# A recurrent outer-product layer with a maxout network on one core: a new list of steps, output weights in packets of two rows, GpSimd steps tied to the list, and the last span's operands turned by transfers

## Chip, core and metric

The kernel runs on one core of a Trainium2 chip. The metric is the device time of one execution in microseconds, as the median of several runs. Engines are named as in the profile: PE (TensorE), PEld (its weight loads), DVE (VectorE), ACT (ScalarE), POOL (GpSimd), SP (SyncE, which here issues the transfers). Each takes its instructions from its own queue, in order. Matmuls write PSUM, which has 8 banks here, each of 512 float32 in 128 partitions.

## What is computed

Four batches, eight heads, 768 time steps, 48 features a head. A gated recurrence makes y; its heads side by side (384 columns) are the input of a small network:

```python
f = 1.0 / (1.0 + np.exp(-f_logit))
for t in range(S):
    state = f[:, :, t, :, None] * state + np.einsum('bhd,bhe->bhde', k[:, :, t], v[:, :, t])
    y[:, :, t] = np.einsum('bhd,bhde->bhe', q[:, :, t], state)
x = y, as 3072 rows of 384
out = np.maximum(x @ w1, x @ w2) @ w_out      # w1, w2: 384 x 1024, w_out: 1024 x 384
```

Everything is float32 in memory. The kernel uses max(a, b) = relu(a - b) + b: with wd = w1 - w2 and m2 = w2 @ w_out, out = relu(x @ wd) @ w_out + x @ m2.

## The kernel before

Time is cut into three windows of 256 steps, each in two halves of 128 steps, and a "span" s (0 to 11) is one window of one batch: window s // 4, batch s % 4. A partition holds two neighbouring time steps (the "parities"), so 64 partitions hold a half. Of each span four arrays f, k, q, v are loaded, 384 KB each, into 27 slots of one tile (line 122, packets of 384 bytes: two steps of one head).

The whole program is a list of words, `ORDER` (lines 20 to 58). The loop in lines 541 to 543 takes each word apart into a step, its numbers, the engine (a, v, p, s for ACT, DVE, POOL, SP) and the PSUM bank after the @, and calls the step's function. So the list gives each engine the order of its queue. What one engine needs of another is a semaphore wait that the framework derives from the tiles. The instructions stay in the list's order; nothing plans again at build time.

The steps of one span, in the order of the data:

- Lf, Lk, Lq, Lv: the loads (SP). E, F, G: the gate's exponential and logarithm (ACT, lines 211 to 221). e: sum of the two parities' logarithms (line 223). C: running sums by a triangular matmul (PE, line 226). X, Z: their exponentials (ACT).
- i, j: k and q of the even step times the gate. K, Q: keys and queries scaled to the start of the half, in bf16 (lines 257, 260). V: cast of v (line 264). These run on DVE or POOL, V also on ACT.
- t, u: 16 + 16 transposes of keys (t) and queries (u) on PE (line 268) into two banks. U: their copy to SBUF, tile `trs` (line 279).
- A: keys times queries within a half (line 284). m: that product times the causal mask, on DVE (line 297). D: the state that a half adds (line 378). n, N: the state after a half and its decay (lines 401, 408).
- S, z, y: PE adds what the state gives (S, line 327) and what the half itself gives (y, line 359) in two banks; z is a one-column copy by DVE in between, so that PE and DVE agree on S's end.
- Y: copy of y to SBUF. For spans 0 to 5 and 11 y is written transposed (tile `xT`). Spans 6 to 10 ("TURNED") write it untransposed into `xr`, of which there is one buffer, and M (line 425) is a transposing transfer on SP that makes `xT`.
- d0 to d3: x @ wd, 6 matmuls each (line 431). r: relu to bf16, tile `gT` (line 439). o: the output for one parity, 3 matmuls with m2 and 8 with w_out (line 449). b: copy of the result to SBUF. O: the store (line 468), for TURNED spans two transfers.

The weights have their own steps. Wa0 to Wa3: quarters of w1's columns, 384 KB each. Wb0 to Wb2: rows of w2, 512 KB each. Wo0, Wo1: halves of w_out, 768 KB each. ws: one quarter of wd, w1 - w2 (line 509), which needs all of w2. wc, wt, wx: cast, transpose and copy of w2. wo: casts of w_out. wm, wn: m2 and its copy. g: zeroes of a state buffer.

The list lets PE begin with spans 0 and 1 and the weights; then spans follow each other with the steps of neighbours interleaved.

Of the kernel before, what the change touches and what calls it, by code (L numbers as in the profile page):

```python
# [27 lines left out]
wo2p wo3a d1.1@3 r1.1v@6 Z2 wm0@0 X2 g6v Lk4s@22 r1.0a@2 i2v wm1@1 K2v Lf5s@23 j2v wm2@2 Q2v Lq4s@24  # L28
E3 wn1v@1 t2@4 u2@4 F3 U2.0v@4 Lf6s@12 V2p wn2a@2 wn0v@0 o0.1@1 U2.1v@5 e3p A2.1@2 Lq5s@13 b0.1.0a@1
D2@4 A2.0@6 G3 n2.0v C3@0 j3v o1.1@1 Z3 n2.1v Lk5s@0 i3v X3 Q3v o1.0@0 m2.1v@2 E4 K3p F4 m2.0v@6  # L30
b1.1.0a@1 S2.0@2 V3p u3@4 z2v@2 t3@4 e4p S2.1 y2 U3.2v@4 D3@6 Y2.2a@2 C4@1 n3.0v N2.1v A3.0@4 G4
n3.1v A3.1@2 m3.0v@4 E5 o0.0@6 i4p F5 m3.1v@2 Z4 d2.2@4 X4 e5v G5 j4v S3.0@2 b0.0.0a@6 d2.3@5 K4v E6
O0.2s C5@1 Lq6s@1 d2.1@7 z3v@2 r2.1a@4 Q4v Lv4s@2 S3.1 y3 Lk6s@3 F6 j5v Lf7s@4 N3.1v t4@4 X5 Y3.2v@2
i5p u4@4 Lv6s@5 Z5 d2.0@6 U4.2v@4 e6p d3.1@3 r2.0a@6 d3.0@2 g7p K5v G6 C6@1 d3.2@4 r3.0a@2 Q5v
d3.3@5 Z6 j6v X6 t5@2 u5@2 Q6v r3.1a@4 o2.1@1 U5.2v@2 V4a i6p b1.0.0a@0 O1.2s A4.1@2 K6p D4@4
m4.1v@2 A4.0@6 Lv5s@6 E7 o3.1@0 Lf8s@7 F7 Lq7s@8 n4.0v m4.0v@6 Lf9s@9 N4.0p e7p Lq9s@10 t6@2
# [12 lines left out]
r7.0a@4 N9.0v i10p Lv10s@24 d8.3@7 O6.2s X10 d8.1@5 r7.1a@2 K10v d8.2@6 d8.0@4 r8.1a@6 o7.1@1
r8.0a@4 j10v Q10p S9.0@2 t11@4 t10@6 z9v@2 u11@4 S9.1 y9 U11.0v@4 u10@6 U11.1v@5 o7.0@0 U10.2a@6  # L50
V11v V10v b7.1.0v@1 o8.1@4 Y9.2a@2 b7.0.0a@0 M9s D10@1 b8.1.0a@4 D11@0 O7.2s A11.0@2 A10.0@6 n11.0v
A11.1@4 m10.0v@6 o8.0@0 m11.1v@4 d9.0@6 N11.0v n10.0v d9.1@7 m11.0v@2 N10.0p d9.3@5 r9.0a@6 d9.2@4
b8.0.0v@0 O8.2s S10.0@0 r9.1a@4 S11.0@2 z10v@0 A10.1@6 z11v@2 S11.1 y11 m10.1v@6 S10.1 y10 Y11.0a@2
Y11.1a@3 o9.0@4 Y10.2a@0 M10s d11.2@5 b9.0.0v@4 d11.1@0 d11.3@1 o9.1@4 d10.1@3 b9.1.0v@4 r11.4a@5
# [6 lines left out]
M2_LAST = (0,)  # L61
TURNED = (6, 7, 8, 9, 10)


@with_exitstack
def kernel(
# [196 lines left out]

    def step_V(s, e):
        copy(e, pad("vb", s)[:, :, :, 0:D], by_parity(loaded[s]["v"]))


    def transposes(s, x, b):
        src = pad("kpqp"[2 * x:2 * x + 2], s)
        for j in range(NP):  # L270
            for par in range(2):
                for h in range(2):
                    rows = slice(h * HC, (h + 1) * HC)
                    ps = banks16[:, b + h, :].rearrange("p (x j a t) -> p x j a t", x=2, j=NP, a=2)
                    nc.tensor.transpose(out=ps[:, x, j, par, :],  # L275
                                        in_=src[rows, par, 2 * j:2 * j + 2, :].rearrange("p r e -> p (r e)"),
                                        identity=ident[rows, rows])
# [49 lines left out]
    def step_S(s, part, b):  # L327
        t = tr[s]
        if s in TURNED:
            ys[s] = b if part == 0 else ys[s]  # L330
            for j in range(NP):
                for r in range(2):
                    h = r if part else 1 - r
                    if has_state(s, h):
                        rows = slice(r * DP, r * DP + D)
                        add_turned(s, h, 2 * j + r, t[rows, h, 1, j].rearrange("p a t -> p (a t)"),
# [131 lines left out]
    def step_O(g, part):  # L468
# [3 lines left out]
        if g in TURNED:  # L472
            dst = out[row:row + W, :].rearrange("(h t a) m -> a t h m", h=2, a=2)
            for a in range(2):
                nc.sync.dma_start(out=dst[a], in_=obs[g][a * HC:(a + 1) * HC])
            return
        if g == n_s - 1 and part > 0:
            cols = slice((part - 1) * HD // 2, part * HD // 2)
            nc.sync.dma_start(out=dst[:, 1, cols], in_=obs[g][:, 1, cols])
            return  # L480
        pars = slice(0, 2) if part == 2 else slice(part, part + 1)
        nc.sync.dma_start(out=dst[:, pars, :], in_=obs[g][:, pars, :])


    def cast_w2(kt, e):
        copy(e, w2b[:, kt, :], w2_f[:, kt, :])
# [22 lines left out]
    def subtract(part, e):  # L509
        cols = slice(part * d_ff // 4, (part + 1) * d_ff // 4)  # L510
        engines[e].tensor_sub(wd[:, :, cols], w1_f[:, :, cols], w2_f[:, :, cols])
# [13 lines left out]
        "t": lambda s, e, b: transposes(s, 0, b), "u": lambda s, e, b: transposes(s, 1, b),  # L525
        "U": lambda s, i, e, b: step_U(s, i, e, b),
# [3 lines left out]
        "Y": lambda s, i, e, b: step_Y(s, i, e, b), "g": lambda i, e, b: step_g(i, e), "M": lambda s, e, b: step_M(s, e),  # L530
        "D": lambda s, e, b: step_D(s, b),
# [3 lines left out]
        "O": lambda s, i, e, b: step_O(s, i),  # L535
# [38 lines left out]
```

## Time and profile before

| what | us |
| --- | --- |
| median of three runs | 140.69 (140.13, 140.69, 142.11) |
| the profiled execution | 141.23 |
| its span, first to last instruction | 139.5 |
| busy PE, PEld, DVE, ACT, POOL | 119.1, 89.5, 101.7, 79.0, 45.3 |
| transfers: bytes, mean rate over the span | 29.65 MB, 213 GB/s |

The profile is of one execution. Its times count from the first instruction of the span, in microseconds; the 1.73 us between span and time lie outside. In a timeline row come start, duration, engine, line, operation, tiles and count, and in square brackets how long the engine had been idle and what ended that. In a row by form come the total busy time, the mean of one in nanoseconds, and the idle time ahead of such instructions. A row of stretches gives the stretch, its length, the busy time of the five engines, the granted clock, the share of the 16 DMA engines and GB/s. PE's busy time is modelled in part, since matmuls are pipelined: a busy PE may not be at its peak.

### The profile page before, as it was taken

The page shows a single profiled execution, that of the slowest core. Times are in us where ns is not written, and L with a number is a line of the kernel's source. Part 1 is how long each engine was busy: PE and PEld are TensorE (multiplying, and loading weights), DVE is VectorE, ACT ScalarE, POOL GpSimd, SP SyncE. Part 2 cuts the span into 40 slices and gives each one's busy share as a digit, 9 for nine tenths or more (in the row PEclk, how much of TensorE's full clock was granted, in tenths as well). Part 3 has the DMA queues.
Part 4 walks back from the last instruction along what each step waited for, and adds up shares of the span by engine and source line. Part 5 has one row for each costly group of instructions (what it writes and reads, how often), then busy time and mean ns, then how long its engine had stood idle before and what let it go on. Part 6 is the DMA issues. An engine that isn't in the chain of part 4 may idle for free. (4 is left out here: it accounts for less than half of the span.)

```text
span 139.5 us, 5551 instructions
## 1 busy us (share of the span) xinstructions
PE 119.1 (85%) x2455; PEld 89.5 (64%) x2455; DVE 101.7 (73%) x173; ACT 79.0 (57%) x120; POOL 45.3 (32%) x52
## 2 busy tenths in 40 slices
PE   0045489599999999999999699989999999999991
PEld 0024377586567687677787566776877668778671
DVE  5687798999889999989974989982642768312630
ACT  3784349665592996973983355693675814504301
POOL 5003007640538224482073096719635001000000
PEclk9999999999999999999999999999999999999999
DMA  4999999999999989999999999909899461422124
GB/s 109 271 261 296 348 332 349 369 267 251 269 265 257 271 222 273 239 248 250 247 297 222 224 274 163 288 30 96 121 260 313 130 140 34 118 56 61 57 62 164
DMA packets 59768, 29.65 MB, mean 213 GB/s; under 512 B 54368, under 2 KB 58592, under 8 KB 59744
## 3 DMA queue, kind: packets, MB, share of 16 engines
q1 hardware_dynamic: 59744, 29.30, 87.5%
q8 instruction: 19, 0.31, 1.0%
q14 instruction: 5, 0.04, 0.1%
HBM read 23.59 MB, written 4.72 MB: 203 GB/s over the span
## 5 line engine op out<-in xcount | busy, mean ns | idle before, releaser
L436 PE MATMUL banks<-xT,wd 128*128 128x256 bf16 x288 | 34.7, 273 | 2.3 <-DVE xT L114 2.0
L461 PE MATMUL banks<-wo,gT 128*128 128x384 bf16 (+1 forms) x200 | 35.3, 320 | 0.0
L436 PEld LDWEIGHTS <-wd 128*128 128x128 bf16 x288 | 27.2, 98 | 6.9 <-issue 2.3
L445 ACT ACTIVATE gT<-banks 128x1024 bf16<-128x1024 f32 (+1 forms) x20 | 19.5, 982 | 20.2 <-PE banks L436 15.7
L299 DVE TENSOR_TENSOR at_m<-banks,mask 128x1024 bf16<-128x1024 f32 x24 | 28.8, 1218 | 0.8 <-PE banks L292 0.5
L461 PEld LDWEIGHTS <-gT 128*128 128x128 bf16 x200 | 19.2, 98 | 11.8
L247 POOL TENSOR_TENSOR slots<-slots,one 128x384 f32<-128x384 f32 x8 | 8.5, 1058 | 28.1 <-DMA slots<-in_k_dram 18.3
L461 PE MATMUL banks<-m,xT 128*128 128x384 bf16 (+1 forms) x75 | 15.9, 320 | 0.0
L114 ACT COPY ob<-banks 128x384 f32<-128x384 f32 (+1 forms) x16 | 7.4, 460 | 11.9 <-PE banks L461 11.9
L114 DVE COPY trs<-banks 128x2048 bf16<-128x2048 bf16 (+1 forms) x12 | 11.9, 997 | 2.4 <-PE banks L275 2.3
L213 ACT ACTIVATE gate<-slots 128x768 f32<-128x768 f32 x12 | 10.1, 841 | 5.0 <-DMA slots<-in_f_logit_dram 5.0
L114 DVE COPY ob<-banks 128x384 f32<-128x384 f32 x9 | 5.0, 555 | 8.9 <-PE banks L461 8.9
L228 PE MATMUL banks<-e,u_inc 128*128 128x384 bf16 x12 | 4.2, 354 | 8.0 <-DVE e L224 8.0
L258 POOL TENSOR_TENSOR kp<-slots,inv 128x768 bf16<-128x768 f32 x5 | 9.6, 1913 | 3.0 <-DVE slots L247 2.9
L404 DVE TENSOR_TENSOR tmp_s<-banks,state 128x192 f32<-128x192 f32 x16 | 5.6, 352 | 6.7 <-ACT ob L114 3.9
L217 ACT ACTIVATE ell<-gate 128x768 f32<-128x768 f32 x12 | 10.1, 845 | 0.2
L292 PE MATMUL banks<-trs 48*64 48x128 bf16 x384 | 10.1, 234 | 0.0
L261 POOL TENSOR_TENSOR qp<-slots,dec 128x768 bf16<-128x768 f32 x4 | 7.3, 1817 | 8.3 <-PE banks L314 4.9
L251 DVE SCALAR_TENSOR_TENSOR slots<-gate,slots 128x384 f32<-128x384 f32 x12 | 6.6, 552 | 3.9 <-DMA slots<-in_q_dram 3.9
L114 ACT COPY trs<-banks 128x1024 bf16<-128x1024 bf16 (+1 forms) x4 | 4.8, 1227 | 7.0 <-PE banks L275 7.0
L292 PEld LDWEIGHTS <-trs 48*64 48x64 bf16 x384 | 7.5, 115 | 1.6 <-issue 1.1
L461 PEld LDWEIGHTS <-xT 128*128 128x128 bf16 x75 | 6.5, 97 | 3.2
(73 smaller groups left out, 186.3 us busy)
## 6 DMA issues: line engine op xcount, KB each, us to landing
slots<-in_f_logit_dram SPq DMA_DIRECT2D x12, 384.0 KB, 6.4
slots<-in_q_dram SPq DMA_DIRECT2D x12, 384.0 KB, 6.2
slots<-in_k_dram SPq DMA_DIRECT2D x12, 384.0 KB, 6.1
slots<-in_v_dram SPq DMA_DIRECT2D x12, 384.0 KB, 5.8
out_dram<-ob SPq DMA_DIRECT2D x6, 384.0 KB, 3.9
out_dram<-ob SPq DMA_DIRECT2D x11, 192.0 KB, 3.4
slots<-in_moe_w_dram SPq DMA_DIRECT2D x4, 384.0 KB, 8.7
slots<-in_moe_w_dram SPq DMA_DIRECT2D x3, 512.0 KB, 8.8
```

Of the source, the lines that this page charges most:

```text
L114: (nc.scalar.copy if e == "a" else engines[e].tensor_copy)(out, in_)
L213: nc.scalar.activation(flat(gate[s]), flat(loaded[s]["f"]), AF.Exp, bias=0.0, scale=-1.0)
L217: nc.scalar.activation(flat(ell[s]), flat(gate[s]), AF.Ln, bias=1.0, scale=1.0)
L247: engines[e].tensor_mul(even, even, one[s])
L251: engines[e].scalar_tensor_tensor(out=even, in0=gate[s][:, :, 1, :], scalar=1.0, in1=even, op0=ALU.add, op1=ALU.mult)
L258: engines[e].tensor_mul(pad("kp", s)[:, :, :, 0:D], by_parity(loaded[s]["k"]), both(inv[s]))
L261: engines[e].tensor_mul(pad("qp", s)[:, :, :, 0:D], by_parity(loaded[s]["q"]), both(dec[s][:, 0:HD].rearrange("p (h d) -> p h d", h=H)))
L292: nc.tensor.matmul(out=ps[h * HC:(h + 1) * HC, j % 2, par, :], lhsT=t[rows, h, 0, j, par, :], rhs=t[rows, h, 1, j].rearrange("p a t -> p ( ...
L299: nc.vector.tensor_mul(at[s][:, jj].rearrange("p r j a t -> p (r j) (a t)"), banks[:, b:b + 2, :].rearrange("p r (j x) -> p (r j) x", j=2) ...
L436: nc.tensor.matmul(out=ps[:, f], lhsT=wd[:, kt, ff * C:(ff + 1) * C], rhs=xT[g][:, kt], start=(kt == 0), stop=(kt == KT - 1))
L445: nc.scalar.activation(dst, src, AF.Relu)
L461: nc.tensor.matmul(out=ps, lhsT=lhs, rhs=rhs, start=(i == 0), stop=(i == len(terms) - 1))
```

## The change

All of `ORDER` is new, 578 words for 574. What it does:

- The loads at the start come as f0, f1, k0, Wb2, q0, q1, v0, f2, Wb0, Wb1, k1, Wa1, Wa0, v1, Wa3, Wa2, Wo1, f3, Wo0 (before: f0, f1, q0, k0, k1, v0, q1, Wa2, Wb1, v1, Wb2, Wb0, f2, Wa0, Wa3, Wa1, Wo0, Wo1). The steps behind them are rearranged; those for keys of span 0 now come ahead of its queries.
- Steps change engine. For instance DVE makes 8 of the K (7 before), 10 of the e (6), 7 of the i (4), 7 of the N (9), and 6 of the U copies (12); ACT makes 10 of the U (4), all wn and five of the V (3); POOL has 2 of the e (6), 5 of the i (8), 4 of the K (5), 9 of the N (7) and 2 of the ws (1).
- The queries of spans 0 and 1 are made by halves of the heads (q), turned by halves (uq), and copied in parts (U with numbers 3 to 5: all keys, the first or the second half of the queries).
- The output weights are loaded with two neighbouring rows in one packet of 3072 bytes (1536 before). So partition p of a pair of feature blocks holds features 2p and 2p + 1, and w1 and w2 have to be dealt in the same way: `cast_w2` and `subtract` read every second column.
- A step of the kinds in `SHARED` on POOL gets a dependency on the last listed step of these kinds on DVE.
- Span 11's keys and queries are turned by two transfers on SP (Mk, Mq, 256 KB each) in place of t11, u11 and two U11 copies; A11 and S11 read the other layout.
- O7, O8, O9 and the last part of O11 are issued by ACT.

```diff
 ORDER = """
-Lf0s@16 g0v Lf1s@17 Lq0s@18 Lk0s@19 Lk1s@20 Lv0s@21 Lq1s@22 Wa2s E0 Wb1s F0 Lv1s@23 E1 e0v C0@0 F1
-Wb2s j0v Z0 e1v X0 Q0v G0 C1@1 Wb0s i0v X1 u0@2 G1 g2v K0v Lf2s@24 i1p t0@2 U0.0v@2 U0.1a@3 Wa0s V0v
-Z1 K1v D0@2 A0.1@0 Wa3s j1v A0.0@4 Q1v Wa1s m0.1v@0 u1@6 t1@6 Wo0s n0.0v U1.0a@6 U1.1a@7 Wo1s V1v
-n0.1v D1@0 m0.0v@4 S0.0@2 A1.0@6 Lk2s@25 wc2a z0v@2 m1.0v@6 A1.1@4 S0.1 y0 Lq2s@26 wc0a ws2p n1.0v
-n1.1v m1.1v@4 S1.0@6 Y0.0a@2 wt2@0 Lf3s@16 E2 g5p z1v@6 N1.1v S1.1 y1 N0.1p Lv2s@17 g3p ws0v wt0@1
-Y1.1a@7 wx2a@0 Y0.1v@3 wc1p Lq3s@18 Y1.0v@6 d0.2@2 F2 g1p ws3v d0.0@4 Lk3s@19 wx0a@1 wt1@0 g4v e2v
-d0.3@3 ws1v C2@1 r0.1a@2 d1.2@6 Lf4s@21 wo0v wx1v@0 wo1p d0.1@5 G2 d1.3@7 r0.0v@4 d1.0@2 Lv3s@20
...
+Lf0s@16 g5p g7v g3v Lf1s@17 g2p Lk0s@18 g0p Wb2s Lq0s@19 Lq1s@20 Lv0s@21 Lf2s@22 E0 Wb0s F0 Wb1s E1
+e0v C0@0 F1 Lk1s@23 G0 X0 i0v G1 Wa1s wc2v Z0 K0v e1v Wa0s t0@0 j0v wt2@2 U0.3v@0 Lv1s@24 q0.0v C1@3
+j1v uq0.0@0 q0.1v Wa3s V0v uq0.1@0 U0.5a@0 wx2v@2 U0.4a@0 A0.1@4 Z1 Wa2s A0.0@0 m0.1v@4 X1 q1.0p E2
+Wo1s g6p q1.1v m0.0v@0 g4p uq1.1@2 uq1.0@2 U1.5a@2 wc0p D0@4 Lf3s@25 F2 n0.0v S0.0@0 Wo0s z0v@0 i1p
+n0.1v S0.1 y0 N0.1p Lq2s@26 K1v wt0@4 Y0.1a@1 wc1a U1.4v@2 ws1v t1@2 wt1@5 U1.3a@2 e2v Lk2s@16 ws0v
+C2@6 wx0a@4 A1.1@2 Y0.0v@0 Lv2s@17 V1p wx1v@5 d0.0@0 m1.1v@2 d0.1@1 Lk3s@18 ws3p A1.0@4 r0.0a@0 D1@2
+m1.0v@4 Lq3s@19 Z2 ws2p d0.3@1 G2 n1.0v X2 n1.1v S1.0@4 z1v@4 S1.1 y1 Lv3s@21 wo2v d0.2@0 Y1.0v@4
+Y1.1a@5 wo3p Lf4s@22 E3 d1.3@3 d1.1@5 F3 d1.2@2 e3v d1.0@4 Lf5s@20 wo1a wo0v C3@7 r0.1v@0 r1.0a@4
...
 M2_LAST = (0,)
+SHARED = ("e", "i", "j", "K", "Q", "q", "V", "N", "ws", "wc", "wo")
 TURNED = (6, 7, 8, 9, 10)
+BY_DMA = (11,)
...
-        engines[e].dma_start(out=wo_f[:, part, :],
-                             in_=moe_w_out.rearrange("(j p) m -> p j m", p=C)[:, part, :])
+        engines[e].dma_start(out=wo_f[:, part, :].rearrange("p (g two) m -> p g (two m)", two=2),
+                             in_=moe_w_out.rearrange("(g p two) m -> p g (two m)", p=C, two=2)[:, h * FG // 4:(h + 1) * FG // 4, :])
...
+    def step_q(s, jj, e):
+        hs = slice(4 * jj, 4 * jj + 4)
+        sums = dec[s][:, 0:HD].rearrange("p (h d) -> p h d", h=H)[:, hs]
+        engines[e].tensor_mul(pad("qp", s)[:, :, hs, 0:D], by_parity(loaded[s]["q"])[:, :, hs],
+                              sums.unsqueeze(1).to_broadcast([C, 2, 4, D]))
...
     def step_U(s, part, e, b):
         t = tr[s] = buf("trs", s, 3, [C, 2, 2, NP, 2, HC], BF16)
+        if part > 2:
+            x, js = (0, slice(0, NP)) if part == 3 else (1, slice(2 * part - 8, 2 * part - 6))
+            src = banks16[:, b:b + 2, :].rearrange("p h (x j y) -> p h x j y", x=2, j=NP)
+            copy(e, t[:, :, x, js].rearrange("p h j a t -> p h (j a t)"),
+                 src[:, :, x, js].rearrange("p h j y -> p h (j y)"))
+            return
...
+    def step_turn(s, x, e):
+        t = tr[s] = buf("trs", s, 3, [C, 2, 2, NP, 2, HC], BF16)
+        src = pad("kpqp"[2 * x:2 * x + 2], s).rearrange("p two h e -> p (two h e)")
+        engines[e].dma_start(out=whole(t)[:, x], in_=src, transpose=True)
...
     def cast_w2(kt, e):
-        copy(e, w2b[:, kt, :], w2_f[:, kt, :])
+        copy(e, w2b[:, kt, :].rearrange("p (g f m) -> p g f m", f=2, m=C),
+             w2_f[:, kt, :].rearrange("p (g m f) -> p g f m", f=2, m=C))
...
     def subtract(part, e):
         cols = slice(part * d_ff // 4, (part + 1) * d_ff // 4)
-        engines[e].tensor_sub(wd[:, :, cols], w1_f[:, :, cols], w2_f[:, :, cols])
+        w1, w2 = (t[:, :, cols].rearrange("p k (m f) -> p k f m", f=2) for t in (w1_f, w2_f))
+        engines[e].tensor_sub(wd[:, :, cols].rearrange("p k (f m) -> p k f m", f=2), w1, w2)
...
+    ahead = None
     for word in ORDER.split():
         key, of, e, b = re.fullmatch(r"([A-Za-z]+)([0-9.]+)([avps]?)@?([0-9]*)", word).groups()
         steps[key](*map(int, of.split(".")), e, int(b or 0))
+        if key in SHARED and e in ("v", "p"):
+            ins = nc.cur_bb.bb.instructions[-1]
+            if e == "v":
+                ahead = ins.name
+            elif ahead:
+                tc.add_manual_dep(ins, ahead, mybir.DependencyInfo(mybir.DependencyClass.Sync,
+                                                                   mybir.DependencyReason.DATA),
+                                  reason="as listed")
```

The queue of DVE in the new list from the first weight cast to the end of span 1 is: wc2, K0, e1, j0, U0.3, q0.0, j1, q0.1, V0, wx2, m0.1, q1.1, m0.0, n0.0, z0, n0.1, K1, U1.4, ws1, e2, ws0, Y0.0, wx1, m1.1, m1.0, n1.0, n1.1, z1. PE's, up to the point of which the prediction speaks: C0, t0, wt2, C1, uq0.0, uq0.1, A0.1, A0.0, uq1.1, uq1.0, D0, S0.0, S0.1, y0, wt0, t1, wt1, C2, A1.1, d0.0, d0.1, A1.0, D1, d0.3, S1.0, S1.1, y1, d0.2.

Later in the list, PE's queue behind span 10's y is o9.1, S11.1, y11, o9.0, d10.2; and between K11 and A11.1 it has D9, A9, o7.0, the four d8, S9, y9, o7.1, A10.1 and D11.

More of the change, by code (lines that the diff above doesn't have):

```diff
@@ L31 @@
[L31 to L36, printed above, removed]
@@ L49 @@
[L49 to L54, printed above, removed]
@@ L58 @@
+r9.0a@4 N10.0v b8.0.0a@2 S10.0@0 S11.0@4 z10v@0 A11.0@6 S10.1 y10 m11.0v@6 o9.1@2 Y10.2a@0 z11v@4
+b8.1.0a@3 M10s S11.1 y11 b9.1.0a@2 O8.2a o9.0@3 Y11.0v@4 Y11.1v@5 d10.2@0 b9.0.0a@3 d10.1@5 d10.0@4
+d11.1@2 r10.0a@4 d11.3@3 O9.2a d10.3@1 d11.0@4 r10.1v@0 d11.2@5 o10.0@6 r11.4a@5 r11.2a@4 r11.3a@2
+r11.5a@3 o10.1@5 b10.0.0v@6 o11.0@2 b10.1.0v@5 O10.2s o11.1@3 b11.0.0v@2 O11.0s o11.2@2 b11.1.1v@3
+O11.1s b11.1.2a@2 O11.2a
 """
 M2_LAST = (0,)
+SHARED = ("e", "i", "j", "K", "Q", "q", "V", "N", "ws", "wc", "wo")
@@ L335, in step_S @@
                         rows = slice(r * DP, r * DP + D)
+                        if s in BY_DMA:
+                            for a in range(2):
+                                nc.tensor.matmul(
+                                    out=banks[a * HC:(a + 1) * HC, ys[s] + h, (2 * j + r) * D:(2 * j + r + 1) * D],
+                                    lhsT=query_t(s, rows, h, j)[:, a], rhs=heads_of(state_before(s, h))[rows, j, :],
+                                    start=(s, h, a) not in begun, stop=False, skip_group_check=True)
+                                begun.add((s, h, a))
+                            begun.add((s, h))
+                            continue
                         add_turned(s, h, 2 * j + r, t[rows, h, 1, j].rearrange("p a t -> p (a t)"),
```

86 lines of the change are left out of this document (51 added, 35 removed).

## The prediction

> **What bounds the kernel now.** I read the page's busy shares and slices first, then busy time in chosen stretches, then the timeline of the first 30 us, and last the rows by form and the times to landing.
>
> ```profile
> PE 119.1 (85%) x2455; PEld 89.5 (64%) x2455; DVE 101.7 (73%) x173; ACT 79.0 (57%) x120; POOL 45.3 (32%) x52
> ...
> PE   0045489599999999999999699989999999999991
> ...
> GB/s 109 271 261 296 348 332 349 369 267 251 269 265 257 271 222 273 239 248 250 247 297 222 224 274 163 288 30 96 121 260 313 130 140 34 118 56 61 57 62 164
> ```
>
> TensorE is filled from about the ninth slice on; in the first eight it is not. In stretches (columns: length, then busy us of PE, PEld, DVE, ACT, POOL):
>
> ```profile
> 0.00:28.51 28.51, 13.63 (x370) 11.82 (x371) 23.12 (x55) 16.30 (x23) 7.89 (x19) 1.00 1.07 293
> 28.51:90.00 61.49, 59.79 (x1308) 43.57 (x1306) 55.87 (x86) 40.96 (x66) 27.23 (x26) 1.00 1.09 249
> 90.00:130.00 40.00, 39.12 (x736) 29.60 (x734) 20.31 (x33) 20.57 (x29) 10.14 (x9) 1.00 0.57 129
> 130.00:139.50 9.50, 6.56 (x52) 4.49 (x49) 2.37 (x5) 1.13 (x4) 0.00 (x0) 1.00 0.28 83
> ```
>
> PE idles 14.9 us of its 20.4 before 28.51, 1.7 and 0.9 us in the next 101.5 us, and 2.9 us at the end, where the last eviction and the last store follow the last matmul. So the end moves only if PE gets work earlier, gets less work, or loses time it does not lose now. A gain on DVE, ACT, POOL or a queue counts only through one of these. The granted clock is 1.00 throughout.
>
> Why 28.51: there d1.2 starts, and from there PE hardly waits.
>
> ```profile
> 4.45 0.84 ACT L213 ACTIVATE gate<-slots 128x768 f32<-128x768 f32 x1 [2.44 <-DMA slots<-in_f_logit_dram]
> ...
> 7.46 0.56 DVE L251 SCALAR_TENSOR_TENSOR slots<-gate,slots 128x384 f32<-128x384 f32 x1 [0.70 <-DMA slots<-in_q_dram]
> ...
> 20.15 1.05 ACT L114 CAST slots<-slots 128x1024 bf16<-128x1024 f32 x1 [1.94 <-DMA slots<-in_moe_w_dram]
> ...
> 21.68 1.82 POOL L511 TENSOR_TENSOR wd<-slots 128x768 bf16<-128x768 f32 x1 [9.93 <-DMA slots<-in_moe_w_dram]
> ...
> 28.51 3.43 PE L436 MATMUL banks<-xT,wd 128*128 128x256 bf16 x30
> ```
>
> The same for DVE alone:
>
> ```profile
> 12.21 0.55 DVE L114 CAST vb<-slots 128x768 bf16<-128x768 f32 x1
> 12.67 0.95 DVE L258 TENSOR_TENSOR kp<-slots,inv 128x768 bf16<-128x768 f32 x1
> 13.54 0.55 DVE L251 SCALAR_TENSOR_TENSOR slots<-gate,slots 128x384 f32<-128x384 f32 x1
> 14.20 0.96 DVE L261 TENSOR_TENSOR qp<-slots,dec 128x768 bf16<-128x768 f32 x1
> 15.07 1.22 DVE L299 TENSOR_TENSOR at_m<-banks,mask 128x1024 bf16<-128x1024 f32 x1
> 16.21 0.35 DVE L406 TENSOR_TENSOR state<-banks,dec 128x192 bf16<-128x192 f32 x1
> 17.37 0.56 DVE L114 CAST vb<-slots 128x768 bf16<-128x768 f32 x1 [0.81 <-DMA slots<-in_v_dram]
> ...
> 22.48 1.23 DVE L409 TENSOR_TENSOR state<-tmp_s,dec 128x192 bf16<-128x192 f32 x1
> 24.18 1.03 DVE L511 TENSOR_TENSOR wd<-slots 128x768 bf16<-128x768 f32 x1 [0.47 <-DMA slots<-in_moe_w_dram]
> ```
>
> By 28.51 PE has done C0 to C2, all of t, u, A, D, S and y of spans 0 and 1, the three wt, and three d steps (d0.2, d0.0, d0.3). In the new list PE has done exactly this set, with d0.0, d0.1, d0.3, when it comes to d0.2, the step behind y1. So one question decides the head: when does d0.2 start? Call it T; the head costs T - 28.51 more than now.
>
> **The change, part by part.**
>
> *The new order of the head.* From the landing of the first W rows to the `look` of span 1 (z1), DVE has one queue of 28 steps, and PE's steps hang on them in turn. DVE steps overlap a little, so I use start-to-start times from the rows above: K 0.87 (12.67 to 13.54), m 1.14 (15.07 to 16.21), V cast 0.46 (12.21 to 12.67), and the rest from these rows, shortened by 0.08 (the 384-column steps 0.46 by the row at 13.54):
>
> ```profile
> L114 DVE COPY trs<-banks 128x1024 bf16<-128x1024 bf16 x5 | 3.4, 688 | 1.5 <-PE banks L275 1.5
> ...
> L511 DVE TENSOR_TENSOR wd<-slots 128x768 bf16<-128x768 f32 x3 | 2.9, 973 | 0.5 <-DMA slots<-in_moe_w_dram 0.5
> ...
> L114 DVE CAST xT<-banks 128x384 bf16<-128x384 f32 x2 | 1.0, 544 | 0.0
> ```
>
> Landings: the first load is there at 4.45, the third at 7.46, so 1.5 us for each 0.393 MB. Wb2 (0.524 MB) is now fourth: 7.5 + 1.8 = 9.3; DVE's next step in the list, its cast wc2, waits for it, with K0, e1 and all else behind. Then: wc2 0.61 (V's time for 1024 columns), K0 0.87, e1 0.46, j0 0.5, U0.3 0.61, q0.0 0.46, j1 0.5, q0.1 0.46, V0 0.46, wx2 0.6 end at 14.8. A0.1 has to wait for its queries through uq0.1 and U0.5a, so m0.1 starts near 15.3 (now 15.07). m0.1 1.14, q1.1 0.46, m0.0 1.14, n0.0 0.4, a hop over S0.0, z0 and n0.1 end at 19.4.
>
> K1 is next and needs i1 on GpSimd, which needs k1, now the eleventh load. Up to it lie 4.72 MB; rows of before, with the loads summed (384 and 512 KB): 4.06 MB at 17.37, 4.59 at 20.15, 5.11 at 21.68. At 1.5 us a load k1 lands near 20.3, i1p adds 1.1, so K1 starts at 21.5: DVE idles 2 us. Then K1 0.87, U1.4 0.35, ws1 0.9, e2 0.46, ws0 0.9, Y0.0 0.47, wx1 0.6, m1.1 1.14 end at 27.1; d0.0, d0.1, A1.0 lie on PE beside them, the last until 27.4. m1.0 1.14, two n, S1 and y1 (1.3 us) end at 30.2. The weights keep up: ws1 and ws0 come at 22.8 and 24.1, for 5.11 and 5.5 MB; ws3p and ws2p (1.82 each) end by 29.5, before d0.2. So T is 30.2 without contention.
>
> *GpSimd held to the list.* A POOL step among the listed kinds now waits for the DVE step listed before it; nothing holds the DVE step behind it. Behind i1p on POOL stand N0.1p, V1p (y1 needs it), ws3p and ws2p (d0.3 and d0.2): V1 is loaded by 24, so they end in time as above. The row at 22.48 shows what an overlap costs: 1.23 us where this form takes 0.35, until the 1.82 us POOL subtraction ends at 23.50. N0.1p comes free together with K1 (both behind i1p): 0.5 us by POOL's own row.
>
> ```profile
> L409 POOL TENSOR_TENSOR state<-tmp_s,dec 128x192 bf16<-128x192 f32 x7 | 3.8, 546 | 11.2 <-DVE tmp_s L404 11.2
> ...
> L114 POOL CAST vb<-slots 128x768 bf16<-128x768 f32 x3 | 2.5, 825 | 7.0 <-DMA slots<-in_v_dram 7.0
> ```
>
> V1p beside e2 could cost 0.8 more. I take 0.5: T = 30.7. [...]
>
> *Span 11's keys and queries by transfer* removes 32 transposes from PE. In the chain of waits, 48 of them take 0.70 us, so 32 are 0.47 us. It also takes two DVE copies of 0.69 us where DVE is loose.
>
> ```profile
> 107.03 0.70 PE banks L275 x48
> ```
>
> The landings of M6 to M10 (768 columns):
>
> ```profile
> DMA to landing us min/median/max: 2.8/3.8/5.4
> ```
>
> Two transfers of 1024 columns join SP behind M8, with O4 between them; by the median they should take 5.1. PE has D9, two A, two o, four d, y9 and more (over 9 us) before A11.1: hidden. Without that cover it would cost up to 5 us. The part's bounds are -0.47 and +5.
>
> *Later transfers.* M10 is covered by o9.1, S11, y11 and o9.0, some 4.9 us, against 0.8 for Y10 and 3.8 for the landing; hidden by 0.3, and the slowest landing would stall PE by 1.3 us. I take 0.
>
> *Output weights in packets of two rows*: the same 1.57 MB in half the packets. wm2, their first use on PE, stands behind all of d1, later than now; hidden, 0. The features dealt to block pairs make the subtractions and w2 casts read every second column; no row shows that. Bounds: 0, and a doubling (ws1 and ws0 0.9 each, wc2 0.6). I take 0, as these steps already run at about one column a nanosecond. *Halved Q and U copies* are in the head's sum. *Stores on ACT*: seven issues leave SP for ACT, among its last evictions. No row shows ACT issuing; SP's take 0.8 each:
>
> ```profile
> 104.18 1.61 SPq L475 DMA_DIRECT2D out_dram<-ob  x2
> ```
>
> ACT has 20.6 us busy in the 40 up to 130, so 0; the bound is 1.6, if the four r11 were late behind O9.2's two issues.
>
> *Sum against the profiled execution* (141.23 us: span 139.5, 1.73 around it): 139.5 + (30.7 - 28.5) - 0.47 = 141.2, with 1.73: 143.0. That run stands 0.54 above the median of 140.69; taken as a difference of +1.7, I predict 142.4.
>
> **The rivals.**
>
> 1. *The head comes as early as now, and the middle tightens.* k1 lands by 19.1 (4.06 MB at 17.37 and 0.66 MB at the page's best 0.37 MB/us), no lock: T = 29.0. And PE's 2.6 us of idle time between 28.51 and 130 go, as six of DVE's twelve U copies go to ACT while DVE is at 55.87 of 61.49. Time: 140.69 + 0.5 - 0.47 - 2.6 = 138.1. Against it: all of it has to go, which a filled list seldom allows.
> 2. *Collisions make DVE the bound in the middle* (slower). POOL has 27.23 us of work between 28.51 and 90, DVE 5.6 us of room. Held steps start together with the next DVE step; if those with two SBUF inputs wait for a whole POOL step more than 5.6 us in all, PE starves. Counted from the new list by the groups' means, POOL keeps about 21 us there; half of it blocking is 10.5, so 10.5 - 5.6 = 4.9 us, and DVE's lighter load gives about 2 back: +2.9 on the forecast, 145.3. For it: the 22.48 row. Against it: the middle of before shows POOL and DVE busy together with PE losing 1.7 us.
> 3. *The head changes nothing*: POOL and loads fall as now and T is 28.5; -0.47, 140.2. The dealt reads at double price lie on the other side: T + 2.4, 144.8.
>
> **How the numbers follow.** Forecast 0.5 (its own range 140.7 to 143.9: T from 29.0 to 32); rival 1 0.1; rival 2 0.22; no change in the head 0.12; dealt reads slow 0.06. The range, 139.4 to 145.3, leaves most of rival 1 and the upper half of rival 2 outside. Two per cent, about what a measurement of this kernel can tell from no change, is 2.8 us: 137.9 to 143.5. Faster takes half of rival 1 (0.05). Slower takes rival 2, the slow reads (most of 0.28: 0.25) and an eighth of the forecast (0.06): 0.31. The rest, 0.64, is the same.
>
> **What would show it.** Right: d0.2 starts at 30 to 32; DVE idles about 2 us ahead of K1, waiting for POOL's i1, and that for k1; PE idles some 2 to 3 us between T and 130; transposes 352. Wrong: d0.2 before 29, or DVE's steps with two SBUF inputs stretched in the middle, PE idle there over 5 us. A subtraction on DVE much over 0.97 us would show the dealt reads' price.

## The result, and the profile after

The changed kernel took 147.31 us (median of 4, 145.94 to 147.66) against 140.41 us before (median of 4): a ratio of 1.0497, 95% interval 1.0392 to 1.0602. It is slower by 6.9 us; 142.4 was predicted, at most 145.3. Some executions fall into a slower state (one of four of the kernel with quarters, below, took 144.41 us, the others 141.12 to 141.72); the medians here are of all executions, the ratios and their intervals of the others alone. The profiled execution took 145.94 us with a span of 144.1 us, 1.4 us below the median (that of before lay 0.5 to 0.8 above its own).

The page, busy times and slices:

```profile
PE 121.1 (84%) x2423; PEld 89.8 (62%) x2423; DVE 100.8 (70%) x174; ACT 85.1 (59%) x126; POOL 37.3 (26%) x47
...
PE   0116684296999999999999999999999999999991
...
PEclk9999999659999999999999999999999999999999
```

PE has the 32 matmuls less that the transfers take (x2455 before), and from the eleventh slice on it shows nothing but 9 up to the last one, where before still shows an 8 or a 6 at times. But slices 7 and 8, where before has 9 and 5, are at 4 and 2, and in slices 8 and 9 the granted clock falls to 6 and 5. In stretches (length; then PE, PEld, DVE, ACT, POOL busy; then clock), cut where d0.2 starts, the moment that the prediction called T:

```profile
0.00:36.10 36.10, 17.07 (x370) 13.00 (x370) 22.91 (x55) 15.65 (x24) 12.99 (x24) 0.91 1.06 285
36.10:144.10 108.00, 104.04 (x2059) 76.76 (x2054) 77.89 (x119) 69.49 (x102) 24.26 (x24) 1.00 0.79 184
```

T is 36.10, not 30.7: the head costs 7.6 us more than before. Behind T the kernel needs 108.0 us where before needs 111.0 (139.5 - 28.51). All of the loss lies ahead of T. The timelines of DVE, POOL and PE there:

```profile
15.15 1.22 DVE L328 TENSOR_TENSOR at_m<-banks,mask 128x1024 bf16<-128x1024 f32 x1 [0.64 <-PE banks L323]
...
19.95 1.25 DVE L260 TENSOR_TENSOR kp<-slots,inv 128x768 bf16<-128x768 f32 x1 [0.44 <-POOL slots L249]
21.12 0.41 DVE L116 COPY trs<-banks 128x512 bf16<-128x512 bf16 x1
26.34 0.96 DVE L551 TENSOR_TENSOR wd<-slots 128x768 bf16<-128x768 f32 x1 [4.81 <-DMA slots<-in_moe_w_out_dram]
```

```profile
28.70 0.82 POOL L116 CAST vb<-slots 128x768 bf16<-128x768 f32 x1 [8.32 <-DVE wd L551]
29.49 4.27 POOL L551 TENSOR_TENSOR wd<-slots 128x768 bf16<-128x768 f32 x2
```

```profile
27.82 0.48 PE L230 MATMUL banks<-e,u_inc 128*128 128x384 bf16 x1 [4.52 <-DVE e L226]
...
29.16 2.72 PE L474 MATMUL banks<-xT,wd 128*128 128x256 bf16 x12 [0.20 <-DVE xT L116]
...
36.10 3.51 PE L474 MATMUL banks<-xT,wd 128*128 128x256 bf16 x30
```

Up to U1.4 at 21.12 the head goes as forecast or faster (m0.1 at 15.15, K1 at 19.95). Then DVE stands still for 4.81 us before ws1, the first subtraction. Everything behind it in DVE's queue is late by as much: e2, and so PE's C2, which waits 4.52 us; ws0, for which the held V1p waits 8.32 us on POOL though its data are there by 24 (the same cast starts at 24.05 in the kernel with quarters, below). The row names the output weights as releaser, and that is the wrong name. By their view (line 146 on SP) the first of these two transfers is issued at 19.2, and none lands in under 9.0 us, so not before 28.2, when ws1 was already done:

```profile
L146 SPq DMA_DIRECT2D slots<-in_moe_w_out_dram x2: 954/2276/3597, 19.2 to 21.0; - x2
...
DMA to landing us min/median/max: 9.0/9.8/10.6
```

What ws1 waits for can be read from the program. The rows are the waits of the DVE subtractions in before (ws0, ws3, ws1), in the changed kernel (ws1, ws0) and in the changed kernel with the reads undealt; each name is a semaphore on which a transfer counts its landing:

```
before   [waits DMAHW3_49,DMAHW5_49,DMAHW2_49,DMAHW0_49]  [waits DMAHW6_49]  [waits DMAHW7_49]
changed  [waits DMAHW4_49,DMAHW6_49,DMAHW3_49,DMAHW7_49,DMAHW1_49,DMAHW0_49]  (none)
undealt  [waits DMAHW3_49,DMAHW1_49,DMAHW0_49]  [waits DMAHW4_49]
```

Before, each subtraction waits for one quarter of w1, the first also for the rows of w2. In the changed kernel DMAHW4, 6, 3 and 7 stand for Wa0, Wa3, Wa1 and Wa2, DMAHW1 and 0 for Wb1 and Wb0. So the first subtraction there waits for all four quarters, three more than undealt, and the second for nothing new. No load of w_out is in the list. But Wo1 counts on DMAHW0 as well, behind Wb0, and this is probably how it came into the row. The view of line 139, the four loads of w1's quarters on SP (duration of one issue in ns, least, median and most, then the first and the last start):

```profile
L139 SPq DMA_DIRECT2D slots<-in_moe_w_dram x4: 732/1017/2247, 12.4 to 18.2; - x4
...
DMA to landing us min/median/max: 7.6/7.8/9.2
```

The last, Wa2, is issued at 18.2; with the median landing that gives 26.0, and its own landing in the trace is at 26.2. ws1 starts at 26.34. My theory: the dealt read ("p k (m f) -> p k f m") makes the dependency cover all of w1's slots, so ws1 waits for four quarters in place of its own. Rivals: the dealt elements or the packets are slow in themselves; the hold is what costs.

### The profile page after: what moved, and what is told of

The parts are those of the page before. It is cut to its first block, busy times and chain, and to the rows that moved or that the text cites. A ratio compares the mean times of both kernels' runs of the same rounds, so it can differ in the third digit from the quotient of the medians.

```text
span 144.1 us, 5487 instructions
## 1 busy us (share of the span) xinstructions
PE 121.1 (84%) x2423; PEld 89.8 (62%) x2423; DVE 100.8 (70%) x174; ACT 85.1 (59%) x126; POOL 37.3 (26%) x47
## 4 chain that ended last, share of the span: by engine, by line
PE 66%; SPq 12%; DVE 8%; DMA 5%; ACT 4%; POOL 1%; issue 1%; DVEq 0%; POOLq 0%
PE banks L499 26%; PE banks L474 22%; SPq L127 7%; DMA slots<-in_moe_w_out_dram 5%; PE banks L344 5%; SPq L139 3%; PE banks L323 3%; PE banks L352 3%; PE banks L283 2%; DVE trs L116 2%; SPq L142 2%; PE banks L542 2%; PE banks L425 2%; DVE wd L551 1%; POOL qp L263 1%; ACT trs L116 1%
## 5 line engine op out<-in xcount | busy, mean ns | idle before, releaser
L474 PE MATMUL banks<-xT,wd 128*128 128x256 bf16 x288 | 35.3, 279 | 0.3 <-DVE xT L116 0.2
L474 PEld LDWEIGHTS <-wd 128*128 128x128 bf16 x288 | 27.9, 100 | 5.2 <-issue 0.3
L499 PEld LDWEIGHTS <-gT 128*128 128x128 bf16 x200 | 19.2, 98 | 11.8
L116 ACT COPY trs<-banks 128x2048 bf16<-128x2048 bf16 (+2 forms) x10 | 13.0, 1314 | 5.9 <-PE banks L283 5.9
L233 PEld LDWEIGHTS <-e 128*128 128x128 bf16 x48 | 3.2, 102 | 10.8 <-issue 9.9
L485 DVE TENSOR_SCALAR gT<-banks 128x1024 bf16<-128x1024 f32 x5 | 6.1, 1221 | 5.3 <-PE banks L474 5.3
L263 POOL TENSOR_TENSOR qp<-slots,dec 128x768 bf16<-128x768 f32 x3 | 5.4, 1816 | 16.5 <-DVE slots L253 11.5
L260 POOL TENSOR_TENSOR kp<-slots,inv 128x768 bf16<-128x768 f32 x4 | 7.3, 1815 | 9.3 <-DVE qp L263 6.8
L116 DVE COPY ob<-banks 128x384 f32<-128x384 f32 (+1 forms) x10 | 5.3, 535 | 6.1 <-PE banks L499 6.1
L260 DVE TENSOR_TENSOR kp<-slots,inv 128x768 bf16<-128x768 f32 x8 | 7.9, 989 | 0.6 <-POOL slots L249 0.4
L447 POOL TENSOR_TENSOR state<-tmp_s,dec 128x192 bf16<-128x192 f32 x9 | 4.8, 535 | 13.7 <-DVE tmp_s L442 5.8
```

What stands on the lines that cost most here:

```text
L116: (nc.scalar.copy if e == "a" else engines[e].tensor_copy)(out, in_)
L260: engines[e].tensor_mul(pad("kp", s)[:, :, :, 0:D], by_parity(loaded[s]["k"]), both(inv[s]))
L263: engines[e].tensor_mul(pad("qp", s)[:, :, :, 0:D], by_parity(loaded[s]["q"]), both(dec[s][:, 0:HD].rearrange("p (h d) -> p h d", h=H)))
L474: nc.tensor.matmul(out=ps[:, f], lhsT=wd[:, kt, ff * C:(ff + 1) * C], rhs=xT[g][:, kt], start=(kt == 0), stop=(kt == KT - 1))
L499: nc.tensor.matmul(out=ps, lhsT=lhs, rhs=rhs, start=(i == 0), stop=(i == len(terms) - 1))
```

## Experiments

**Undealt weights.** The changed kernel with the packets and the reads of before.

```
-  w1, w2 = (t[:, :, cols].rearrange("p k (m f) -> p k f m", f=2) for t in (w1_f, w2_f))
-  engines[e].tensor_sub(wd[:, :, cols].rearrange("p k (f m) -> p k f m", f=2), w1, w2)
+  engines[e].tensor_sub(wd[:, :, cols], w1_f[:, :, cols], w2_f[:, :, cols])
   (and likewise load_wo and cast_w2)
```

> The changed kernel with the output weights in packets of one row again, and the subtractions and w2 casts reading every column in order; list, hold and the last span's transfers stay. Theory W (the dealt read makes the first subtraction on DVE wait for all four quarters of w1, the last of which lands near 26.2): the first DVE subtraction starts near 22 instead of 26.3, d0.2 near 31 instead of 36.2, and the time falls by 5 us from the changed kernel's 147.3, to 141 to 143. Rival H (the hold of GpSimd steps keeps V1 and two subtractions back) and rival L (the list itself is late in the head): d0.2 stays at 35 or later, the time at 146 or more.

Measured 142.36 us (1.0184, 1.0103 to 1.0266). DVE, POOL and PE:

```profile
21.60 0.94 DVE L549 TENSOR_TENSOR wd<-slots 128x768 bf16<-128x768 f32 x1
```

```profile
25.14 3.58 POOL L549 TENSOR_TENSOR wd<-slots 128x768 bf16<-128x768 f32 x2 [0.33 <-DMA slots<-in_moe_w_dram]
```

```profile
30.77 3.51 PE L474 MATMUL banks<-xT,wd 128*128 128x256 bf16 x30
```

T is 30.77, the forecast's 30.7. So packets, dealing or their wait are the miss; the list, the hold and the transfers of span 11 are not, as all three are still in this kernel.

**Quarters.** All of the change, but each quarter of w1 has its own stretch of the slots, so that a dealt read covers its own quarter alone.

```
-  w1_f = staged(0, KT)       # then dst[:, :, cols] for quarter i
+  w1_f = staged(0, 4)        # then dst[:, i], a quarter's KT rows of columns in one stretch
+  w1 = w1_f[:, part].rearrange("p (k m f) -> p k f m", k=KT, f=2)
```

> The changed kernel with all its parts, but w1 is laid in its slots quarter by quarter, so that a subtraction's read covers its own quarter alone; the dealt reads and the two-row packets stay. Theory W: as without the dealing, d0.2 near 31 and 141 to 143 us, within 1 us of that run. If instead the price lies in reading every second column, d0.2 stays at 34 or later and the time at 145 or more, though the wait is gone. Rivals H and L: 146 or more.

Measured 141.47 us (1.0128, 1.0016 to 1.0239). ws1's list of waits is again three names. DVE, POOL and PE:

```profile
21.35 0.94 DVE L553 TENSOR_TENSOR wd<-slots 128x768 bf16<-128x768 f32 x1
```

```profile
24.05 0.82 POOL L116 CAST vb<-slots 128x768 bf16<-128x768 f32 x1 [3.77 <-DMA slots<-in_v_dram]
...
25.21 4.29 POOL L553 TENSOR_TENSOR wd<-slots 128x768 bf16<-128x768 f32 x2 [0.34 <-DMA slots<-in_moe_w_dram]
```

```profile
24.38 1.48 PE L475 MATMUL banks<-xT,wd 128*128 128x256 bf16 x12
...
27.43 0.83 PE L475 MATMUL banks<-xT,wd 128*128 128x256 bf16 x6 [0.97 <-POOL wd L553]
...
30.22 3.51 PE L475 MATMUL banks<-xT,wd 128*128 128x256 bf16 x30
```

The loss is gone with packets and dealing in place. A dealt subtraction costs DVE nothing (0.94 both ways) and POOL 0.35 us (4.29 for two against 3.58); PE waits 0.97 us for it, ahead of d0.3, and T is none the later than in the undealt kernel.

**The wait alone.** The undealt kernel, whose subtractions are made to wait for all four quarters. Its list of waits is then that of the changed kernel.

```
+  for name in quarters:       # the four transfers of w1
+      tc.add_manual_dep(nc.cur_bb.bb.instructions[-1], name, ..., reason="all quarters")
```

> The changed kernel without two-row packets and dealt reads (142.4 us), to which one thing is added: each subtraction waits for all four quarters of w1, as the changed kernel's does. Theory (that wait alone is the loss; how the elements are read is not): the first subtraction at 26.2 to 26.4 instead of 21.6, the 30 matmuls of d0.2 and d1 4 to 5.5 us later, 146 to 147.5 us, as the changed kernel. Rival (the wait would be absorbed, and the loss is the dealt reads running beside GpSimd): 142 to 144 us.

Measured 147.32 us (1.0496, 1.0443 to 1.0549), against 147.31 for the changed kernel. DVE and PE:

```profile
26.33 0.96 DVE L551 TENSOR_TENSOR wd<-slots 128x768 bf16<-128x768 f32 x1 [4.71 <-DMA slots<-in_moe_w_out_dram]
```

```profile
36.09 3.51 PE L476 MATMUL banks<-xT,wd 128*128 128x256 bf16 x30
```

The wait by itself gives the whole loss, at the same place to 0.01 us. And the profile again names the output weights, where the added wait is for w1 and nothing else was added: here the releaser named for a wait on several transfers was a guess, and a wrong one.

**Without the hold.** The changed kernel without the dependency that ties POOL's steps to the list (the block behind `if key in SHARED` is removed).

> The changed kernel without the dependency of GpSimd steps on the DVE steps listed before them. Theory W: the first DVE subtraction still starts at 26.3; V1 on POOL moves from 28.7 to about 24.5 and the two POOL subtractions to about 26.3, so d0.3 and d0.2 wait less: d0.2 near 34 to 35, 145 to 147 us. Rival H: d0.2 near 31, 141 to 143 us.

Measured 151.78 us (1.0853, 1.0763 to 1.0944), 4.5 us more than with it; neither number was near. DVE and POOL:

```profile
26.18 0.96 DVE L551 TENSOR_TENSOR wd<-slots 128x768 bf16<-128x768 f32 x1 [4.84 <-DMA slots<-in_moe_w_out_dram]
27.06 2.49 DVE L226 TENSOR_TENSOR e<-ell 128x384 bf16<-128x384 f32 x1
29.47 2.91 DVE L551 TENSOR_TENSOR wd<-slots 128x768 bf16<-128x768 f32 x1
```

```profile
26.22 5.35 POOL L551 TENSOR_TENSOR wd<-slots 128x768 bf16<-128x768 f32 x2 [1.52 <-DMA slots<-in_moe_w_dram]
```

The late quarter frees DVE's ws1 and POOL's ws3 within 0.04 us, and they run into each other: e2 takes 2.49 us where it takes 0.55 with the hold, ws0 2.91 where it takes 0.95. That is 3.9 us for the two, and T, at 39.84, is 3.7 us later than with the hold. With the hold POOL's two start after ws0, and neither step is stretched. So the hold did remove these collisions. In the profiled executions another 2.5 us lies behind T (110.6 us against 108.0), and where it comes from stays open.

**Quarters, without the hold.** Is the hold worth as much without the late quarter?

> The changed kernel with w1 laid quarter by quarter and without the dependency that holds GpSimd's steps to the list. Theory A (the hold keeps GpSimd's dealt subtractions from running beside VectorE's two-input steps, and its worth in the head does not depend on the late quarter): slower than the 141.5 us of the same kernel with the hold by 2 to 4 us, with a VectorE add of span 2 or a subtraction stretched to 2 to 3 us near 22 to 28. Theory B (the 3.7 us were a product of the late quarter, which lined both engines up): within 1 us of 141.5. Theory C (the hold only costs, as waits of GpSimd): 140 to 141 us.

Measured 145.19 us (1.0321, 1.0272 to 1.0370), 3.7 us over the quarters with the hold, as theory A had it; but not for its reason. POOL's subtractions, PE's waits from 26 to 36 (time, count, longest), the clock, and T:

```profile
25.07 4.28 POOL L553 TENSOR_TENSOR wd<-slots 128x768 bf16<-128x768 f32 x2 [0.28 <-DMA slots<-in_moe_w_dram]
```

```profile
PE banks L345 <- issue: 1.3, 1, 1.3
```

```profile
30.00:35.00 5.00, 4.01 (x36) 3.01 (x37) 1.54 (x4) 2.79 (x4) 0.44 (x1) 0.66 1.04 245
```

```profile
31.75 4.75 PE L475 MATMUL banks<-xT,wd 128*128 128x256 bf16 x30
```

The subtractions start as with the hold, and no DVE step is stretched in the head. PE pauses 1.3 us within y1, where the profile shows it waiting for nothing; then the granted clock is 0.66, and the 30 matmuls take 4.75 us, not 3.51. A second pause of 1.3 us without a releaser comes later, in y (line 353). Why they come stays open, and with them what the hold is worth here. (What the clock does is in the last section.)

**Before, with packets and dealing alone; and the same with quarters.** (The second lays w1 out as above.)

> The kernel before, with nothing changed but the two-row packets and the dealing that goes with them. Theory W: the first subtraction (on POOL, 21.7 before) waits for all of w1, to about 27; d0.2 moves from 25.8 to about 30, and the time rises by 3 to 5 us from the kernel before, to 143.5 to 145.5. Without a wait of that kind the two-row packets are hidden: 140.4, within 0.7 us.

> The kernel before, its own list, with the two-row packets and the dealt reads alone, and with w1 laid quarter by quarter in its slots, so that each subtraction can depend on its own quarter only. Theory (all but some tenths of a microsecond of what packets and dealing cost is the wait of the first subtraction for all four quarters): about as fast as before, 140 to 141.5 us, d0.2 within 1 us of 28.5, the two subtractions on GpSimd some 0.35 us longer each, the output-weight transfers hidden either way. Rival (the dealt reads or the packets themselves cost, whatever they wait for): 143 us or more, near the 147.6 of the same edits without the quarters.

The first took 147.57 us (1.0564, 1.0495 to 1.0633), 2 us over the range that was expected; its granted clock is 0.90 on the mean up to T, which the expectation left out. The second took 142.34 (1.0118, 1.0073 to 1.0164). The first subtraction and T in the first:

```profile
26.27 2.92 POOL L513 TENSOR_TENSOR wd<-slots 128x768 bf16<-128x768 f32 x1 [14.47 <-DMA slots<-in_moe_w_out_dram]
```

```profile
34.59 3.44 PE L436 MATMUL banks<-xT,wd 128*128 128x256 bf16 x30
```

and in the second:

```profile
21.48 2.17 POOL L515 TENSOR_TENSOR wd<-slots 128x768 bf16<-128x768 f32 x1 [9.48 <-DMA slots<-in_moe_w_dram]
```

```profile
28.70 3.44 PE L437 MATMUL banks<-xT,wd 128*128 128x256 bf16 x30
```

One edit, and in the old list too the wait is worth 5.2 us. Between them the two lists and the two layouts show the same thing twice. What is left, 1.7 us in the second, was not expected; its T is only 0.2 us late, and where the rest goes is not settled: the two profiled spans differ by 0.4 us alone.

**The transfers alone.** The changed kernel with quarters and span 11 turned by PE again; and the kernel before with span 11 turned by transfers.

```
-  Mq11s ... Mk11s            BY_DMA = (11,)
+  u11@4 t11@4 ... U11.0v@4 U11.1v@5      BY_DMA = ()
```

> The changed kernel with w1 laid quarter by quarter, and span 11's keys and queries turned by TensorE again (32 transposes and two copies put back behind the copy of span 10's). The prediction's term: 0.47 us slower, since TensorE has no idle time there. Rival 1: no difference or faster, since the transfers' landing or the split matmuls of span 11 cost as much. Rival 2: 1 us or more slower, since VectorE's two copies (0.69 us each) come into the chain that ends last.

> The kernel before, with its own list and weights, and only span 11's keys and queries turned by two transfers, in place of 32 transposes and two copies. The prediction's term: TensorE has 0.47 us less work where it has no idle time, so 0.3 to 0.8 us faster. Rival: the transfers land late or the output transfers behind them on SyncE's queue do, and it is no faster, or slower by 1 us and more.

The first took 142.93 us (1.0154, 1.0106 to 1.0203), its span 140.1 against 139.3 with the transfers: the forecast's sign, though the intervals of the two overlap. The second took 141.49 (1.0065, 1.0026 to 1.0104): slower by some 0.6%, where it had been expected 0.3 to 0.8 us faster. PE's wait there, and the landings:

```profile
PE banks L321 <- DMA trs<-qp: 0.9, 1, 0.9
```

```profile
DMA to landing us min/median/max: 5.2/5.8/6.4
```

In the changed list no PE step waits for these transfers; in the old one SP issues the second at 108.35, and PE comes to it 0.9 us too early. So what the part is worth hangs on the work that PE has in between.

**The hold alone, in the kernel before.**

> [...] If the hold is worth what it was worth in the changed list (3.7 us without it there), collisions such as the 1.23 us state update of VectorE beside GpSimd's subtraction go, and it is faster by up to 1 us. If its waits cost more than the collisions in a list made without it: 141 to 144 us.

Measured 140.87 us (1.0021, 0.9985 to 1.0057): no difference that these runs tell. T is 28.33 against 28.51.

**The old head with the new list behind it.** The two lists joined where m2's products are done, weights as before, the hold from there on.

```
before's list up to ... wn1v@1, then: g7v F3 e3v C3@7 G3 ... V2a u2@4 t2@4 Z3 U2.1v@5 wn2a@2 wn0a@0 o0.0@0 ...
mended: ... wn0a@0 E3 wn1v@1 u2@4 t2@4 wn2a@2 g7v F3 U2.1v@5 o0.0@0 e3v C3@7 G3 ... V2a Z3 ...
```

> The list of the kernel before up to the output of m2's products (where TensorE has done d0, d1 and m2), and from there on the changed kernel's list, with span 11 turned by transfers, the hold from there on, and the weights as in the kernel before. Theory (the changed list gains 2 us behind the head and loses in it): d0.2 at 28.5 as before, from there on 109 us as in the changed kernel without the late quarter, so 138 to 139.5 us, faster than both kernels. Rival (the shorter stretch behind the head is work that the longer head had done already, or goes with the loads' order of that head): 140 to 141 us, as before.

> The kernel with the old head and the changed list behind it, its seam mended: span 2's transposes and the first half of o0 now stand ahead of span 3's prefix sum on TensorE, and m2's three copies ahead of the value casts on ScalarE, so that TensorE should not wait the 1.33 and 1.87 us that it waited at the seam (of 141.1 us). Theory (the changed list behind the head is worth some 2 us, and the seam ate it): the span falls by about 3 us, to 138, and the median to 139 to 141 us, as fast as before or somewhat faster. Rival (the list behind the head needs the loads and state of its own head, and new waits come up behind the seam): within 1 us of the 144.5 us with the unmended seam.

144.50 us (1.0250, 1.0177 to 1.0322), and mended 143.56 (1.0230, 1.0187 to 1.0273): by the ratios the mending brought nothing that these runs tell. The first is over both figures that were expected of it (138 to 139.5, the rival 140 to 141). T was 28.37 and 28.33, but from there the span runs another 112.7 and 113.6 us. PE's waits behind the seam, first and second:

```profile
PE banks L498 <- ACT m L115: 1.9, 1, 1.9
PE banks L229 <- DVE e L225: 1.3, 1, 1.3
```

```profile
PE banks L424 <- ACT vb L115: 1.3, 1, 1.3
PE banks L322 <- ACT trs L115: 0.9, 1, 0.9
```

Of the second run's two expectations the rival held: mending one pair of waits brought up another. The 108 to 109 us behind T are no property of that part of the list by itself. In the kernel with quarters POOL has done 12.80 us of work by T, in before 7.89; so the longer head may well pay for part of the shorter rest, though no run shows how much.

## Why the prediction was wrong

*The step that failed* is the sentence "The weights keep up: ws1 and ws0 come at 22.8 and 24.1, for 5.11 and 5.5 MB". It took from the old kernel that a subtraction waits for the bytes it reads, and counted the bytes up to its own quarter. ws1 started at 26.34, because the new form of the read tied it to all four quarters. The same oversight stands in the step on the packets: the dealt reads were costed as time of an element (0 taken, a doubling as the bound), and the diff was not read for what it does to the waits. A price of each element was the wrong kind of bound. With quarters ws1 starts at 21.35, in the undealt kernel at 21.60.

From there the loss of T grew to 5.9 us (36.10 against 30.22 with quarters). 4.99 us are the later start of ws1. Another 1.24 us is the clock, at 0.50 from 26.05 to 32.88: the twelve matmuls of d0.0 and d0.1 take 2.72 us and not 1.48, after PE's 4.5 us of idleness. The two make 6.2; some of it is won back, since d0.3 here does not meet the 0.97 us of waiting that it has with quarters.

*The head without that* was right: 30.77 undealt and 30.22 with quarters, for 30.7. Within it K1 came at 19.95, 1.5 us before the 21.5 forecast, and DVE idled 0.44 us ahead of K1, not 2: k1 landed at 18.9 and not at 20.3. Later steps took that back: with quarters d0.3 waits the 0.97 us for POOL's subtraction ahead of S1, which the forecast had in time, and S1 and y1 take 2.0 us (28.19 to 30.22) for 1.3. So the agreement of T is in part luck: with quarters K1 (at 19.85) is 1.6 us early, what follows takes 1.2 us longer than forecast, and the two mostly cancel.

*The overlap of K1 with N0.1p* was taken at 0.5 us; K1, at 19.95 beside N0.1p at 19.88, took 1.25 where others of its form take 0.95 (0.3).

*"Held steps start together with the next DVE step"*, in rival 2, failed behind K1. A held POOL step need not come free beside the next DVE step of two inputs; here V1p and the two subtractions, from 28.70 and 29.49 on, went behind e2 and ws0 (27.22 and 27.69), and without the hold the changed kernel loses another 4.5 us. In the old list the hold changes nothing.

*The middle* (rival 1's second half) came true unasked: 108.0 us behind T against 110.5 forecast (111.0 less 0.47). From T to 136 PE idles less than 0.9 us, where before idles 2.6 from 28.51 to 130:

```profile
36.10:90.00 53.90, 53.14 (x1159) 38.96 (x1155) 45.95 (x71) 43.78 (x66) 14.09 (x15) 1.00 1.02 243
90.00:136.00 46.00, 45.90 (x862) 34.26 (x861) 30.26 (x46) 25.39 (x36) 10.18 (x9) 1.00 0.60 130
```

Rival 2, PE starved there by collisions of DVE with POOL, is thereby refuted; POOL has 14.1 us of work from T to 90, not the 21 that it counted from 28.51 on. I had given both the wrong places: the gain sat in the middle, the loss in the head.

*The transfers* were hidden, as forecast; their 0.47 us has the right sign in this list.

*The sum.* T 5.4 us over its forecast, the rest 2.5 under: 2.9 us more span. The other 2.0 us of the 4.9 between 147.31 and 142.4 lie in how the profiled executions stand to their medians (0.6 above and 1.4 below).

With the quarters laid apart the kernel takes 141.47 us, inside the range that was given, and still no faster than before (1.0128, 1.0016 to 1.0239).

## What to carry to other kernels

When an edit changes the shape in which an instruction reads a buffer, look first at what the instruction now waits for: a strided view of neighbouring pieces can depend on all of them, and here that cost 5 us where the read itself cost nothing on DVE (0.94 us either way). Lay pieces that arrive separately in separate stretches, and the wait is gone. A wait's releaser in a profile is a candidate: compare the program's waits, and add that wait alone to a kernel that lacks it.

## What the hardware showed beside

The granted clock fell after pauses of PE, in two of the kernels here after pauses of 1.3 us at the most. The rows so far give its mean over longer stretches. Taken finely, the rows have it at 1.00 or 0.50 and nothing between, and a time at 0.50 lasts 3.41, 3.42 or 6.83 us, once or twice the same length. Three pairs of rows show it: the changed kernel, the mended joint kernel, and quarters without the hold. In each pair the first row is the 3.41 us ahead of a fall (after the length comes PE's busy time), the second the time at 0.50:

```profile
22.64:26.05 3.41, 0.62 (x8) 0.51 (x9) 0.00 (x0) 1.93 (x2) 0.00 (x0) 1.00 1.07 372
26.05:32.88 6.83, 4.84 (x81) 3.42 (x81) 4.49 (x6) 0.96 (x2) 4.17 (x3) 0.50 1.14 302
...
38.43:41.84 3.41, 1.25 (x70) 1.06 (x68) 2.13 (x4) 2.51 (x4) 0.41 (x1) 1.00 1.22 266
41.84:45.26 3.42, 3.42 (x11) 1.33 (x10) 2.21 (x2) 2.80 (x4) 1.40 (x1) 0.50 1.18 254
...
27.64:31.05 3.41, 1.79 (x52) 1.16 (x53) 2.02 (x5) 0.86 (x3) 2.80 (x2) 1.00 1.09 336
31.05:34.46 3.41, 3.41 (x31) 2.49 (x32) 1.00 (x2) 2.54 (x4) 0.00 (x0) 0.50 1.03 237
```

The first joint kernel idled more in one piece than the mended one (1.9 us against 1.3) and kept its clock through both of these stretches and behind them:

```profile
34.85:38.26 3.41, 1.83 (x43) 1.25 (x41) 2.19 (x5) 2.82 (x5) 0.00 (x0) 1.00 1.22 266
38.26:41.68 3.42, 1.81 (x11) 0.97 (x10) 2.48 (x4) 2.48 (x5) 0.18 (x1) 1.00 1.25 262
```

So in these rows the length of a pause does not decide it. PE's busy time in such a stretch goes with it: 0.62, 1.25 and 1.79 us came ahead of a fall, 1.81 and 1.83 did not. That puts the border at about 1.8 us of 3.41, an estimate from these five rows alone; PE's busy time is modelled in part, and no run was made to test it.

The prediction read the clock as 1.00 throughout. In the trace of before the record of it begins at 21.84, in that of the changed kernel at 22.64, and the rows print 1.00 ahead of that all the same. The transposes of w2 say otherwise; the rows are wt0 and wt1 of the changed kernel, eight transposes each:

```profile
21.04 1.04 PE L530 MATMUL banks<-ident,slots 128*128 128x128 bf16 x8
...
22.68 0.62 PE L530 MATMUL banks<-ident,slots 128*128 128x128 bf16 x8
```

The same work takes 1.04 us ahead of the first record and 0.62 just behind it. In before one matmul with the state takes 0.31 us at 21.25 and 0.21 at 22.72:

```profile
21.25 0.31 PE L314 MATMUL banks<-trs,state 48*64 48x128 bf16 x1
...
22.72 0.21 PE L314 MATMUL banks<-trs,state 48*64 48x128 bf16 x1
```

So PE most likely ran at a lower clock up to there in both.
